# Transposes of the next token group in one run of eight, and look-ups in runs of four, in an FFT-and-routed-FFN kernel

## The chip, the cores and the metric

One core of a Trainium2 chip runs the whole program. The metric is the device time of one execution in microseconds; the time of a kernel is the median of its runs.

## What is computed

The reference filters eight sequences of 2496 rows by 256 columns in the frequency domain, then sends every filtered row through one of eight experts, each of which takes exactly 2496 rows:

```python
X = np.fft.rfft(x, axis=1)
y = np.fft.irfft(X * F, n=x.shape[1], axis=1).reshape(N, D)      # N = 19968, D = 256
logits = y @ w_gate
for idx in np.argsort(-logits.flatten()):                        # best (token, expert) first
    tok, e = idx // E, idx % E
    if assigned[tok] < 0 and counts[e] < N // E:
        assigned[tok], counts[e] = e, counts[e] + 1
for e in range(E):
    out[assigned == e] = np.maximum(y[assigned == e] @ w1[e], 0) @ w2[e]
```

## The kernel before

The first 400 us are the transforms (class Fft). They leave the filtered rows in device memory (xs) and the gate's logits on chip (lg). From about 420 us on the experts follow one another (class Ffn), and beside each expert the routing for the next ones runs (class Route): one search fixes which expert is closed next and at which logit, and a second part works out which rows belong to it.

**An expert.** Its 2496 rows are gathered by index in 20 tiles of 128 (the last has 64), four tiles to a group, five groups. `gather` issues a group's four indirect transfers on GpSimd's queue into the tiles xg. `turn(e, g, h)` transposes half a group: two tiles of two blocks, four transposes on TensorE (L839) into the PSUM tile ptr, then a cast by ScalarE (L842, hi) and a difference by VectorE (L843, lo), since float32 is carried as a sum of two rounded parts. `first(g, f)` makes one of the eight chunks of a group's hidden layer: six matmuls of up to 512 columns into the PSUM tile pz (L861), ScalarE's Relu into the high part (L867), VectorE's difference into the low part (L869, L872 in the last group). The second layer makes four row tiles per group: 24 matmuls of 256 columns each into py (L904), a copy by ScalarE (L914) and an indirect store (L915). One chunk of the next group stands before the first row tile and one before the fourth (ORD).

pz and ptr share one set of four PSUM buffers, tag "c". In `firsts` the next group is turned in two halves, before chunk 3 and before chunk 5 (TF); the second half is followed by the gather of the group after. The next expert's first group is turned by `hook` in the last group, one half after row tile 1 and one after row tile 2.

**The routing.** `counts` compares the logits with up to nine thresholds (Gm, L553, VectorE), counts by 11 to 13 matmuls (L561) and a few VectorE steps, and sums over partitions by a matmul with ones (L574). Eleven rounds make a search. `places` then finds the rows of the expert that was closed: for each of five pieces of its list, VectorE makes a comparison GE (L764) and four look-ups follow on TensorE (L771), in pairs. A pair writes one tile pr; VectorE takes loc from it (L772), ScalarE sums two Signs (L775, two instructions each), and VectorE takes ex (L776). All these small PSUM tiles have the name "rt" and two buffers, tag "a".

TensorE's order in this stage is the program's order. `Ffn.run` yields after a few matmuls, with the time they take; `Pump.feed` adds that to a clock and lets the routing go on by one step as soon as the step's lag has passed. `yield 'p', LO[2]` in `places` is such a step: the second pair of a piece comes 1.4 us of that clock after the first. The other engines' order is chosen by a scheduler.

Of the kernel before, what the change touches and what calls it, by code (L numbers as in the profile page):

```python
# [21 lines left out]
LAGS = [(1.6, 1.2), (1.9, 1.2), (2.4, 1.4), (2.2, 1.3), (2.2, 1.2), (2.6, 1.2), (2.6, 1.2), (2.6, 1.2)]  # L22
LO, M0, M1, M7 = (2.6, 1.2, 1.4), 3.5, 4.9, 6.9
TU0, TU, PACE = 1.1, 1.15, 5
ORD, TF = (1, 0, 0, 1), (3, 5)
I1, C0 = 5, -2
V1, V1D, V2, V3, VP, AC = 8, 0.5, 3, 2, -1, 6.5
Z0, ZS = 21, 4.6
# [434 lines left out]
class Route:  # L463
# [283 lines left out]
    def places(s, ph, tab, BE, xid, oid):  # L747

        nc, wp = s.nc, s.wb
        v = lambda n, sh, dt=F32, bufs=2: wp.tile(sh, dt, name=n, bufs=bufs)  # L750
        BC, dt = v("BC", [117, 5]), v("dt", [117, 180], F16)
        s.penal(2)
        yield 'o', 1.8
        s.penal(2)
        pd = s.ps.tile([128, 180], F32, name="rt", tag="a", bufs=2)
        nc.tensor.matmul(pd[:117], s.tri[:, 118:], tab, start=True, stop=True)
        nc.vector.tensor_copy(dt, pd[:117])
        ex, loc, js = v("ex", [128, 20, 2]), v("loc", [128, 20]), v("js", [128, 20])
        t1, t7 = v("t1b", [128, 20]), v("t7", [128, 4, 7])
        for ch in range(5):  # L760
            ts = slice(4*ch, 4*ch + 4)
            GE, t2 = v("GE", [117, 512], F16), v("t2", [128, 4])
            nc.vector.tensor_scalar(BC[:, ch:ch+1], BE, -512.0 * ch, None, op0=OP.add)
            nc.vector.tensor_scalar(GE, s.iota, BC[:, ch:ch+1], None, op0=OP.is_ge)  # L764
            yield 'o', LO[0] if ch == 0 else LO[1]
            s.penal(2)
            for t in range(0, 4, 2):
                u = slice(4*ch + t, 4*ch + t + 2)
                pr = s.ps.tile([128, 2, 180], F32, name="rt", tag="a", bufs=2)
                for h in range(2):  # L770
                    nc.tensor.matmul(pr[:, h], GE[:, 128*(t+h):128*(t+h)+128], dt, start=True, stop=True)  # L771
                nc.vector.tensor_tensor(loc[:, u], s.sidx[:, u], pr[:, :, S], op=OP.subtract)  # L772
                for h in range(2):
                    c = 4*ch + t + h
                    nc.scalar.activation(s.junka, pr[:, h, :S], AF.Sign, bias=loc[:, c:c+1], scale=-1.0, accum_out=js[:, c:c+1])  # L775
                nc.vector.tensor_scalar(ex[:, u], pr[:, :, S+1:S+3], MID, None, op0=OP.add)  # L776
                if t == 0:
                    yield 'p', LO[2]
                    s.penal(8)
            nc.vector.tensor_scalar(js[:, ts], js[:, ts], 0.5, S / 2, op0=OP.mult, op1=OP.add)  # L780
            x = nc.vector.scalar_tensor_tensor(xid[:, ts], ex[:, ts, 0], float(S), js[:, ts], op0=OP.mult, op1=OP.add)
            if ch == 0:
                s.last = x.ins
            nc.vector.tensor_tensor(t7, js[:, ts].unsqueeze(2).to_broadcast([128, 4, 7]),
                                    s.k22.unsqueeze(1).to_broadcast([128, 4, 7]), op=OP.is_ge)
            nc.vector.tensor_reduce(t1[:, ts], t7, axis=AX.X, op=OP.add)
            nc.vector.tensor_tensor(t2, js[:, ts], ex[:, ts, 1], op=OP.add)
            nc.vector.scalar_tensor_tensor(oid[:, ts], t1[:, ts], float(N - G), t2, op0=OP.mult, op1=OP.add)
            yield 'g', ch


class Ffn:
# [52 lines left out]
    def run(s, e, pump, hook):  # L845

        nc = s.nc
        ids = pump.out[e]
        out_rows = s.out
        _, ((w1h, w1l), (w2h, w2l)) = s.wt[e]  # L850
        hs = {}

        def first(g, f):
            n = min(512, CAP - 512*g)
            xh, xl = s.xT[e, g]
            p = s.ps.tile([128, 512], F32, name="pz", tag="c", bufs=4)
            m = 0
            for k in range(2):
                sl = slice(1024*k+128*f, 1024*k+128*f+128)
                for w, x in ((w1h, xh), (w1h, xl), (w1l, xh)):  # L860
                    nc.tensor.matmul(p[:, :n], w[:, sl], x[:, k, :n], start=m == 0, stop=m == 5)  # L861
                    m += 1
                yield 0.65 * n / 512
            hl = s.wp.tile([128, 1024], F32R, name="hl", bufs=NH)
            hs.setdefault(g, []).append(hl)
            h, l = (hl[:, 512*k:512*k+512] for k in range(2))
            s.lasta = s.R.relu = nc.scalar.activation(h[:, :n], p[:, :n], AF.Relu).ins  # L867
            if g < 4:
                s.R.low = nc.vector.scalar_tensor_tensor(l[:, :n], p[:, :n], 0.0, h[:, :n].bitcast(F32), op0=OP.max, op1=OP.subtract).ins  # L869
            else:  # L870
                for a, b, c in ((384, n, n), (0, 384, 512)):
                    s.R.low = nc.vector.scalar_tensor_tensor(hl[:, c:c+b-a], p[:, a:b], 0.0, h[:, a:b].bitcast(F32), op0=OP.max, op1=OP.subtract).ins  # L872

        def firsts(g, count):
            for f in range(len(hs.get(g, ())), min(8, len(hs.get(g, ())) + count)):
                if g + 1 < 5:
                    if f == TF[0]:
                        s.turn(e, g + 1, 0)
                    if f == TF[1]:
                        s.turn(e, g + 1, 1)  # L880
                        if g + 2 < 5:
                            hook(('g', g + 2))
                yield from first(g, f)

        hook(('g', 1))
        for g in range(5):
            n = min(512, CAP - 512*g)
            yield from firsts(g, 8)
            if g == 4:
                hook('last')  # L890
            if g == 0:
                hook('w2')
            for t in range(4):
                if g < 4:
                    yield from firsts(g + 1, ORD[t])
                w = min(128, n - 128*t)
                p = s.ps.tile([128, D], F32, name="py", tag="b", bufs=2)
                half = w == 64
                hi, lo, both = slice(128*t, 128*t+w), slice(512+128*t, 512+128*t+w), slice(384, 512)
                terms = ((both, w2h), (hi, w2l)) if half else ((hi, w2h), (hi, w2l), (lo, w2h))  # L900
                m = 0
                for f in range(8):
                    for a, b in terms:
                        nc.tensor.matmul(p[:a.stop-a.start], hs[g][f][:, a], b[:, 256*f:256*f+256],  # L904
                                         start=m == 0, stop=m == 8 * len(terms) - 1, skip_group_check=half)
                        m += 1
                    if f in ((3,) if half else (1, 3, 5)):
                        yield 0.65
                y = s.wp.tile([128, D], F32, name="y", bufs=4)
                if half:  # L910
                    nc.scalar.copy(y[:w], p[w:])
                    nc.vector.tensor_tensor(y[:w], p[:w], y[:w], op=OP.add)
                else:
                    s.lasta = nc.scalar.copy(y, p).ins  # L914
                st = nc.gpsimd.indirect_dma_start(  # L915
                    out=out_rows, out_offset=bass.IndirectOffsetOnAxis(ap=ids[1][:w, 4*g+t:4*g+t+1], axis=0),
                    in_=y[:w], in_offset=None)
                for o in s.scat:
                    s.tc.declare_no_dep(st.ins, o.ins, reason="each token has one place")
                s.scat.append(st)  # L920
                if t in (1, 2) and g == 4:
                    hook(t)
                yield 0.65


def emit(tc, i, out):
    nc = tc.nc
    with ExitStack() as st:
# [100 lines left out]
        with tc.manual_schedule(engines={mybir.EngineType.PE}):  # L1029
            for e in range(8):  # L1030
                pump.limit = e + 1
                def hook(what):
                    if what == 'w2':
                        flush(8)
                    elif isinstance(what, tuple):
                        gather(e, what[1])
                    elif e < 7:
                        if what == 'last':
                            gather(e + 1, 0)
                            flush(4)  # L1040
                        else:
                            W.turn(e + 1, 0, what - 1)
                for pe in W.run(e, pump, hook):
                    pump.feed(pe)
                    n += 1

                    if split and n % PACE == 0:
                        with tc.issue_after(W.lasta):
                            W.split(*split.pop(0))
# [85 lines left out]
```

## Time and profile before

| | us |
|---|---|
| median of three runs | 1422.91 (1422.52 to 1426.01) |
| profiled execution, time | 1421.42 |
| profiled execution, span | 1419.6 |
| TensorE busy | 1377.5 (97%) |
| VectorE busy | 891.6 (63%) |
| ScalarE busy | 673.7 (47%) |
| GpSimd busy | 484.6 (34%) |

The rows come from the profiled execution, whose time is its span and 1.8 us around it. PE is TensorE, PEld its weight loads, DVE VectorE, ACT ScalarE, POOL GpSimd. A matmul's duration runs from its start to the end of its drain; matmuls are pipelined, so what one costs is the distance from its start to the start of the next. The idle time in brackets names what ended it.

### The profile page before, as it was taken

The numbers are of one execution on the slowest core, as the hardware profiler recorded it, in microseconds if no ns is written. First come the engines' busy times: TensorE is split into PE (matmuls) and PEld (weight loads), VectorE is DVE, ScalarE is ACT, GpSimd is POOL, SyncE is SP. The second block draws the span as 40 slices with busy tenths as digits, with TensorE's granted clock in tenths as the row PEclk, the third lists the DMA queues.
The fourth block names the chain that finished last, engine by engine and source line by source line (L and its number), as shares of the span: only waits on it lengthen the run. The fifth ranks groups of instructions, "written<-read, shape, count | busy, mean of one in ns | idle before, by whom it ended". The sixth has DMA issues, their size and how long they took to land.

```text
span 1419.6 us, 27158 instructions
## 1 busy us (share of the span) xinstructions
PE 1377.5 (97%) x10338; PEld 1208.9 (85%) x10338; DVE 891.6 (63%) x2548; ACT 673.7 (47%) x1638; POOL 484.6 (34%) x538
## 2 busy tenths in 40 slices
PE   9999999999959999999999999999999999999998
PEld 8898898976427898898888889889898999899988
DVE  5577676775537778668766876876967635423231
ACT  6766766645454346326325534533623635423232
POOL 3443343431023226323521732433324323323312
PEclk9999999999989999999999999999999999999999
DMA  9665664537881022102212212112111321111100
GB/s 374 242 226 178 209 214 137 155 143 251 300 294 64 31 78 70 44 27 94 62 40 75 68 49 82 53 43 98 50 38 49 127 67 51 47 42 51 40 20 29
DMA packets 56531, 153.10 MB, mean 108 GB/s; under 512 B 9409, under 2 KB 29905, under 8 KB 52817
## 3 DMA queue, kind: packets, MB, share of 16 engines
q1 hardware_dynamic: 28072, 69.46, 14.0%
q0 software_dynamic: 18416, 60.37, 12.9%
q10 hardware_dynamic: 9913, 21.53, 4.3%
q8 instruction: 82, 1.34, 0.4%
q14 instruction: 48, 0.39, 0.1%
HBM read 88.32 MB, written 63.06 MB: 107 GB/s over the span
## 4 chain that ended last, share of the span: by engine, by line
PE 43%; issue 5%; DVE 3%; POOL 1%; ACT 1%; DMA 0%; POOLq 0%; DVEq 0%; ACTq 0%
PE py L904 21%; PE pz L861 19%; PE ptr L839 2%; PE rt L561 1%; POOL out L915 1%; DVE hl L872 1%; PE rt L771 1%; DVE w1l L819 0%; DVE tmp L640 0%; DVE tmp L642 0%; DVE M L638 0%; DVE ar L644 0%; ACT junka L775 0%; ACT hl L867 0%; DMA out<-y,oid 0%
## 5 line engine op out<-in xcount | busy, mean ns | idle before, releaser
L904 PE MATMUL py<-w1h,hl 128*128 128x256 f32 x2496 | 483.8, 286 | 1.0 <-DVE hl L872 1.0
L904 PEld LDWEIGHTS py<-w1h,hl 128*128 128x128 f32 x2496 | 401.7, 191 | 3.6 <-DVE hl L872 1.4
L904 PE MATMUL py<-w1l,hl 128*128 128x256 f32 (+1 forms) x1280 | 358.9, 282 | 0.0
L915 POOL DMA_INDIRECT out<-y,oid x160 | 167.1, 1045 | 496.3 <-ACT y L914 448.3
L867 ACT ACTIVATE hl<-pz 128x512 fp32r<-128x512 f32 (+1 forms) x320 | 187.9, 588 | 230.9 <-PE pz L861 204.1
L861 PE MATMUL pz<-xo,w0h 128*128 128x512 f32 (+1 forms) x640 | 264.2, 413 | 4.0 <-DVE hl L869 2.5
L869 DVE SCALAR_TENSOR_TENSOR hl<-pz,hl 128x512 fp32r<-128x512 f32 x256 | 175.2, 687 | 135.9 <-ACT hl L867 134.6
L861 PE MATMUL pz<-xo,w0l 128*128 128x512 f32 (+1 forms) x640 | 248.9, 389 | 0.0
L861 PE MATMUL pz<-z,w0h 128*128 128x512 f32 (+1 forms) x640 | 248.8, 389 | 0.0
L904 PEld LDWEIGHTS py<-w1l,hl 128*128 128x128 f32 (+1 forms) x1280 | 241.0, 188 | 1.9
L825 POOL DMA_INDIRECT xg<-xs,xid x160 | 170.3, 1064 | 137.1 <-issue 50.6
L914 ACT COPY y<-py 128x256 f32<-128x256 f32 x152 | 56.5, 372 | 298.7 <-PE py L904 264.5
L861 PEld LDWEIGHTS pz<-xo,w0l 128*128 128x128 f32 x640 | 120.9, 189 | 24.1
L861 PEld LDWEIGHTS pz<-xo,w0h 128*128 128x128 f32 x640 | 121.7, 190 | 22.2 <-DVE hl L869 3.0
L861 PEld LDWEIGHTS pz<-z,w0h 128*128 128x128 f32 x640 | 121.8, 190 | 15.7 <-DVE z L843 0.6
L219 ACT COPY Y<-p 64x240 f32<-64x240 f32 (+1 forms) x302 | 115.2, 381 | 30.0 <-PE p L213 22.9
L237 POOL TENSOR_TENSOR P<-P 128x256 f32<-128x256 f32 x80 | 58.6, 732 | 164.0 <-DVE P L235 163.8
L553 DVE TENSOR_TENSOR Gm<-M,thr 117x1232 bf16<-117x1232 f32 (+2 forms) x80 | 105.4, 1328 | 0.2
L213 PE MATMUL p<-cS,xr 117*128 117x120 f32 x688 | 94.0, 276 | 3.4 <-ACT Y L219 1.5
L213 PEld LDWEIGHTS p<-cS,xr 117*128 117x128 f32 x688 | 85.4, 191 | 7.6 <-ACT Y L219 4.3
L229 PE MATMUL p<-cW,Y 128*128 128x128 f32 x640 | 88.4, 276 | 0.6 <-DVE Q L236 0.6
L229 PEld LDWEIGHTS p<-cW,Y 128*128 128x128 f32 x640 | 80.0, 191 | 5.7 <-issue 3.9
(218 smaller groups left out, 1982.3 us busy)
## 6 DMA issues: line engine op xcount, KB each, us to landing
z<-zd SPq DMA_DIRECT2D x26, 600.0 KB
zd<-zt SPq DMA_DIRECT2D x60, 256.0 KB
xs<-xo ACTq DMA_DIRECT2D x18, 600.0 KB
xr<-x SPq DMA_DIRECT2D x6, 1536.0 KB
xr<-x SPq DMA_DIRECT2D x6, 1216.0 KB
zd<-zt ACTq DMA_DIRECT2D x20, 256.0 KB
xs<-xo SPq DMA_DIRECT2D x8, 600.0 KB
xr<-x SPq DMA_DIRECT2D x8, 512.0 KB
```

The costliest lines, as they stand in the source:

```text
L213: s.lastmm = nc.tensor.matmul(p[:, q-q0, :120], xv[:, q-24*h], s.cS1, start=True, stop=True).ins
L219: c = (nc.vector.tensor_copy if (t == 5 if b else cp) else nc.scalar.copy)(dst, src)
L229: nc.tensor.matmul(p[:, k], s.Y1[b][:, 4*g+k, dh*128:dh*128+128], s.cW[:, 4*g+k], start=True, stop=True)
L237: nc.gpsimd.tensor_tensor(P[:, :, :64], P[:, :, :64], P[:, :, 64:], op=OP.subtract)
L553: nc.vector.tensor_tensor(Gm[:, s0:s1, :m], s.M[:, s0:s1].unsqueeze(2).to_broadcast([117, s1 - s0, m]), thr[:117].unsqueeze(1).to_broadcas ...
L825: s.lastg = s.nc.gpsimd.indirect_dma_start(out=xg[:n], out_offset=None, in_=s.xs, in_offset=bass.IndirectOffsetOnAxis(ap=ids[0][:n, t:t+1] ...
L861: nc.tensor.matmul(p[:, :n], w[:, sl], x[:, k, :n], start=m == 0, stop=m == 5)
L867: s.lasta = s.R.relu = nc.scalar.activation(h[:, :n], p[:, :n], AF.Relu).ins
L869: s.R.low = nc.vector.scalar_tensor_tensor(l[:, :n], p[:, :n], 0.0, h[:, :n].bitcast(F32), op0=OP.max, op1=OP.subtract).ins
L904: nc.tensor.matmul(p[:a.stop-a.start], hs[g][f][:, a], b[:, 256*f:256*f+256], start=m == 0, stop=m == 8 * len(terms) - 1, skip_group_check ...
L914: s.lasta = nc.scalar.copy(y, p).ins
L915: st = nc.gpsimd.indirect_dma_start(out=out_rows, out_offset=bass.IndirectOffsetOnAxis(ap=ids[1][:w, 4*g+t:4*g+t+1], axis=0), in_=y[:w], i ...
```

## The change

Three edits. In `places`, the step between the two pairs of a piece is kept for the first search alone (ph is the search's number); in the later seven the four look-ups stand together. In `firsts`, both halves of the next group are turned before chunk 4, and the gather of the group after follows there. At the end of an expert, both halves of the next expert's first group are turned after row tile 1.

```diff
-ORD, TF = (1, 0, 0, 1), (3, 5)
+ORD, TF = (1, 0, 0, 1), 4
...
                 if t == 0:
-                    yield 'p', LO[2]
+                    if ph == 0:
+                        yield 'p', LO[2]
                     s.penal(8)
...
                 if g + 1 < 5:
-                    if f == TF[0]:
-                        s.turn(e, g + 1, 0)
-                    if f == TF[1]:
-                        s.turn(e, g + 1, 1)
+                    if f == TF:
+                        for h in range(2):
+                            s.turn(e, g + 1, h)
                         if g + 2 < 5:
                             hook(('g', g + 2))
...
-                if t in (1, 2) and g == 4:
-                    hook(t)
+                if t == 1 and g == 4:
+                    hook('turn')
...
                         else:
-                            W.turn(e + 1, 0, what - 1)
+                            for h in range(2):
+                                W.turn(e + 1, 0, h)
```

In the changed kernel the lines behind the first edit have numbers one higher, up to `firsts`.

TensorE, a group of the last expert, before, at the second half's transposes (x4 counts equal rows in a row):

```order
L861 MATMUL pz<-xo,w0h 128x512
L861 MATMUL pz<-z,w0h 128x512
L861 MATMUL pz<-xo,w0l 128x512
L839 MATMUL ptr<-id,xg 128x128 x4
L861 MATMUL pz<-xo,w0h 128x512
L861 MATMUL pz<-z,w0h 128x512
```

and in the changed kernel:

```order
L862 MATMUL pz<-xo,w0h 128x512
L862 MATMUL pz<-z,w0h 128x512
L862 MATMUL pz<-xo,w0l 128x512
L840 MATMUL ptr<-id,xg 128x128 x8
L862 MATMUL pz<-xo,w0h 128x512
L862 MATMUL pz<-z,w0h 128x512
```

The two runs of four of a group have become one run of eight.

TensorE at the end of the second expert, before, where the last pair of look-ups but one meets the counts of the next search:

```order
L904 MATMUL py<-w1h,hl 128x256
L771 LDWEIGHTS GE
L771 MATMUL rt<-dt,GE 128x180
L771 LDWEIGHTS GE
L771 MATMUL rt<-dt,GE 128x180
L561 LDWEIGHTS Gm
L561 MATMUL rt<-A,Gm 48x80
```

and in the changed kernel:

```order
L904 MATMUL py<-w1h,hl 128x256
L771 LDWEIGHTS GE
L771 MATMUL rt<-dt,GE 128x180
L771 LDWEIGHTS GE
L771 MATMUL rt<-dt,GE 128x180
L771 LDWEIGHTS GE
L771 MATMUL rt<-dt,GE 128x180
L771 LDWEIGHTS GE
L771 MATMUL rt<-dt,GE 128x180
L561 LDWEIGHTS Gm
L561 MATMUL rt<-A,Gm 48x80
```

The counts now stand behind a run of four.

VectorE in the search beside the fourth expert, before, around a run of transposes (Gm is the search's comparison, hl the eviction of a chunk, z that of a ptr tile):

```order
L594 TENSOR_TENSOR km<-km,di 128x1
L553 TENSOR_TENSOR Gm<-M,thr 117x1232
L869 SCALAR_TENSOR_TENSOR hl<-pz,hl 128x512
L843 TENSOR_TENSOR z<-ptr,xo 128x2x256
L869 SCALAR_TENSOR_TENSOR hl<-pz,hl 128x512
```

and in the changed kernel:

```order
L594 TENSOR_TENSOR km<-km,di 128x1
L553 TENSOR_TENSOR Gm<-M,thr 117x1232
L870 SCALAR_TENSOR_TENSOR hl<-pz,hl 128x512 x2
L844 TENSOR_TENSOR z<-ptr,xo 128x2x256 x2
```

Both chunks that stand ahead of the eight transposes, and both ptr tiles, now follow the Gm.

## Rows read from the trace of the kernel before

**Rows 1.** The page, section 1: busy us, share of the span and instructions per engine.
```profile
PE 1377.5 (97%) x10338; PEld 1208.9 (85%) x10338; DVE 891.6 (63%) x2548; ACT 673.7 (47%) x1638; POOL 484.6 (34%) x538
```

**Rows 2.** Waits of PE, 440 to 1420 us: total us, times, longest.
```profile
PE py L904 <- DVE hl L872: 1.0, 1, 1.0
PE rt L771 <- DVE t L569: 0.9, 1, 0.9
PE rt L561 <- DVE ex L776: 0.6, 2, 0.3
...
PE pz L861 <- DVE hl L869: 0.2, 1, 0.2
```

**Rows 3.** Tile ptr: count, duration min/median/max in ns, first and last start.
```profile
L839 PE MATMUL ptr<-id,xg x320: 222/272/473, 420.2 to 1378.1; 128*128 128x128 f32 x152, 64*128 64x64 f32 x8
```

**Rows 4.** Timeline of PE, 487.1 to 488.8 us: start, duration in us, instruction, count.
```profile
487.60 0.40 PE L861 MATMUL pz<-xo,w0l 128*128 128x512 f32 x1
487.83 0.60 PE L839 MATMUL ptr<-id,xg 128*128 128x128 f32 x4
488.19 0.48 PE L861 MATMUL pz<-xo,w0h 128*128 128x512 f32 x1
488.50 0.39 PE L861 MATMUL pz<-z,w0h 128*128 128x512 f32 x1
```

**Rows 5.** Line 771: count, duration min/median/max in ns.
```profile
L771 PE MATMUL rt<-dt,GE x160: 237/242/375, 400.6 to 1223.8; 117*128 117x180 f16 x160
```

**Rows 6.** Timeline of PE, 652.4 to 653.2 us.
```profile
652.67 0.33 PE L771 MATMUL rt<-dt,GE 117*128 117x180 f16 x2
652.79 0.36 PE L904 MATMUL py<-w1h,hl 128*128 128x256 f32 x1
652.99 0.29 PE L904 MATMUL py<-w1l,hl 128*128 128x256 f32 x1
```

**Rows 7.** Timeline, 686 to 688.2 us, one pair and its readers.
```profile
686.09 0.33 PE L771 MATMUL rt<-dt,GE 117*128 117x180 f16 x2
...
686.46 0.16 DVE L772 TENSOR_TENSOR loc<-sidx,rt 128x2 f32<-128x2 f32 x1 [0.58 <-PE rt L771]
...
687.77 0.16 DVE L776 TENSOR_SCALAR ex<-rt 128x4 f32<-128x4 f32 x1 [0.67 <-ACT junka L775]
```

**Rows 8.** Timeline of PE, 678.3 to 680.3 us, counts right behind a pair.
```profile
679.02 0.58 PE L561 MATMUL rt<-A,Gm 117*48 117x80 bf16 x11 [0.32 <-DVE ex L776]
```

**Rows 9.** Timeline, 1330.6 to 1332 us, eviction of a chunk that ends at 1330.80.
```profile
1330.80 0.60 PE L839 MATMUL ptr<-id,xg 128*128 128x128 f32 x4
1331.00 0.60 ACT L867 ACTIVATE hl<-pz 128x512 fp32r<-128x512 f32 x1 [0.79 <-PE pz L861]
...
1331.63 0.69 DVE L869 SCALAR_TENSOR_TENSOR hl<-pz,hl 128x512 fp32r<-128x512 f32 x1 [0.69 <-ACT hl L867]
```

**Rows 10.** Groups by line, VectorE, 560 to 1420 us: busy us, mean ns, idle before.
```profile
L553 DVE TENSOR_TENSOR Gm<-M,thr 117x1232 bf16<-117x1232 f32 (+1 forms) x50 | 74.0, 1481 | 0.1
```

**Rows 11.** Timeline, 430.3 to 439 us, and the window of the lower clock.
```profile
430.45 0.60 PE L839 MATMUL ptr<-id,xg 128*128 128x128 f32 x4
433.36 0.50 PE L861 MATMUL pz<-xo,w0h 128*128 128x512 f32 x1 [2.31 <-DVE hl L869]
...
435.35 0.68 DVE L869 SCALAR_TENSOR_TENSOR hl<-pz,hl 128x512 fp32r<-128x512 f32 x1
...
438.55 0.48 PE L861 MATMUL pz<-xo,w0h 128*128 128x512 f32 x1
...
434.80:437.80 3.00, 3.00 (x9) 1.98 (x7) 3.00 (x5) 0.60 (x1) 0.00 (x0) 0.51 0.00 0
```

**Rows 12.** Timeline, 664 to 681 us: a gather's issue and the first transposes behind it.
```profile
664.24 0.95 POOL L825 DMA_INDIRECT xg<-xs,xid  x1 [0.30 <-PE py L904]
...
680.35 0.60 PE L839 MATMUL ptr<-id,xg 128*128 128x128 f32 x4
```

**Rows 13.** Window 560 to 690 us: length, busy us of PE, PEld, DVE, ACT, POOL, clock, DMA.
```profile
560.00:690.00 130.00, 128.66 (x934) 113.64 (x933) 93.90 (x308) 56.07 (x142) 52.04 (x47) 1.00 0.19 62
```

## The prediction

> **What bounds the kernel now.** I read the page's totals first: TensorE is busy for 1377.5 us, 97% of the span, no other engine for more than 892 [rows 1]. The change touches the expert stage only, from 420 us on, so I read that stage's waits of TensorE next: between 440 us and the end they come to 3.8 us in seven entries, from 1.0 down to 0.2 [rows 2]. The stage is a queue of matmuls without holes. It follows that an instruction taken from TensorE's queue, or a pause between two kinds of matmul, is worth its full length; that moving work on VectorE, ScalarE or GpSimd is worth nothing by itself; and that any new wait in TensorE's queue is paid in full. So the sum has two sides: what eight in a row and four in a row save between kinds of matmul, and what waits the longer runs make.
>
> **The transposes: almost nothing saved.** There are 320 transposes in 80 calls of turn [rows 3]. The first 8 stand together in both kernels; the other 78 calls become 39 runs of eight. What does one run of four cost? Before the run, matmuls of pz start every 0.23 us (487.60, 487.83); the first transpose starts where the next pz would have; the next pz starts 0.36 us later, and the one behind it another 0.31, 0.08 more than 0.23 [rows 4]. A run of four costs 0.36 + 0.08 = 0.44 us. What of it is the change of kind, which merging saves? The four last 0.60 us together and one lasts 0.272 [rows 3, 4], so they start every (0.60 - 0.272)/3 = 0.109 us, and four times that is 0.437. The rest is nothing to 0.02 us by the rounding of the rows: 39 merges save 0 to 0.8 us. I take 0.2, near the rows' own difference.
>
> Here a rule speaks for a larger gain. The Trainium skill (TensorE: Matmul & The Clock Gate, "Back-to-back issue gap") gives about 81 ns for each matmul of 128 columns in a sustained stream of loads and matmuls; were the added four transposes of each run to settle there, 39 x 4 x (0.109 - 0.081) = 4.4 us would go, by an estimate from that page. The rows show 0.109 from the second transpose on, with no trend that I can see in four, so the sum goes by the rows, and a faster second half is a rival below.
>
> **The look-ups: a small gain.** 160 matmuls of GE make 80 pairs [rows 5]; the ten pairs of the first search stay, 70 pairs become 35 runs of four. A pair between py matmuls, which start every 0.12 us: the next py starts 0.12 after the pair, the one behind it 0.20 after that [rows 6], so a pair costs 0.12 + 0.08 = 0.20 us. The pair lasts 0.33 and one 0.242 [rows 5, 6], so the second starts 0.088 after the first, and two such steps are 0.176; 0.024 is the change of kind. Were the spacing 180 columns at the upper level, 2.4 GHz, or 0.075 us, it would be 0.05. 35 merges save 0.8 to 1.75 us; I take 1.2.
>
> **A new wait: the search's counts behind a run of four.** pr tiles come from the two buffers "rt", which the counts use too. A matmul of counts (L561) needs the buffer used two tiles earlier. Behind a pair that is the pair before, long read; behind a run of four it is the first half of that very run. How long does a pair take to be read? Look-ups at 686.09, loc at 686.46, then two Signs with their accumulator reads, ex from 687.77 to 687.93: 1.84 us [rows 7]. The run of four takes 4 x 0.088 = 0.35 on TensorE, so counts that stand right behind it wait about 1.5 us, and everything in TensorE's queue behind them waits too. The order of the changed kernel has that in two places (at the ends of the first and the second expert), and in three more there are 1.4 us of other matmuls between, which leaves about 0.1 each. That is 2 x 1.5 + 0.3 = 3.3 us new. Against it the old waits of this kind go, since the look-ups of a list now end before the next search's counts begin: 0.9 (look-ups behind the counts' buffer) and 0.6 (counts behind ex) [rows 2]; one of the latter is at 679.02 [rows 8]. Net +1.8 us. Bounds: with waits of the 0.32 us that the old place shows [rows 8], 0.6 - 1.5 = -0.9; with ScalarE held up by a 0.60 us eviction between each pair of Signs and the order twice as unlucky, +4.
>
> **A thinner cover: the buffers of pz.** pz and ptr share four buffers. Before, a run of four stands between chunks 2 and 3 of a group's eight (a chunk is one call of first, six matmuls of 0.23) and another between 4 and 5; the tile that needs its buffer soonest comes 2 x 1.37 + 0.44 = 3.2 us after the end of the one that used it. Now two ptr tiles follow chunk 3, chunks 4 and 5 need the buffers of 2 and 3, and those ended 1.37 + 0.88 = 2.25 us earlier. A quiet eviction takes 1.52 us: a chunk ends at 1330.80, VectorE has subtracted it by 1331.63 + 0.69 [rows 9]. The cover was 1.7 us, now it is 0.73. In the last two experts that costs nothing. While a search runs, VectorE makes a Gm comparison of 1.48 us in ten of a search's rounds, 50 in the five searches from 560 us on [rows 10]. One Gm fits into 1.7, not into 0.73. VectorE's new order puts a Gm right ahead of the one or two evictions before a run of eight in six of the 24 places; a Gm that has just begun makes TensorE wait 1.48 - 0.73 = 0.75, one that is nearly done nothing, so 6 x 0.375 = 2.3 us. Bounds 0 (Gm always early) and 5 (each of the six in full, and the four-buffer delay handed on once). I take 1.9, a little under the mean, since at some of them the Gm starts before the chunk has ended.
>
> **The start of the stage.** TensorE's longest stall, 2.31 us behind VectorE at 431, stands at the first run of four that moves, and the granted clock falls to 0.51 (the lower level, 1.2 GHz) from 434.8 to 437.8, after the stall [rows 11]. Now chunk 3 runs at 430.45 in place of the four, the eight transposes wait for the same evictions, and chunk 4 waits for the eviction that ends at 435.35 + 0.68 = 436.03 [rows 11]. Chunk 4 then ends at 437.4 at full clock or 438.8 at the lower, where before it ended, with its eight transposes, at 438.55. I take -0.5, bounds -1.2 and +0.7.
>
> Nothing else has a price. The last transposes of each expert (after the second y tile of group 4, where they were after the second and the third) find their rows gathered: at the boundary in the rows the fourth of them was issued 16 us ahead of the first transposes [rows 12]. The gather of group g + 2 is issued one chunk sooner on GpSimd's queue, which is 34% busy [rows 1].
>
> **Sum:** -0.2 - 1.2 + 1.8 + 1.9 - 0.5 = +1.8 us on the profiled execution's 1421.42, 1423.2. That execution lies 1.5 under the median of the runs, 1422.91, so the predicted time is **1424.7 us**: no change that a measurement can tell (about 0.3%, 4.3 us, since the runs before spread over 3.5).
>
> **Rivals.** *Faster: the longer runs flow better.* If the second four transposes settle to 128 columns at 2.4 GHz, 0.053 us, the least a run at the clock's upper level can take, 39 x 4 x 0.056 = 8.7 us go: 1414 us. Half of that would be 1418.6. Against it: 0.109 in every run I looked at. A milder way to the same side is that none of the two waits comes and the seven old ones go too: -0.2 - 1.2 - 0.5 - 3.8, 1417.2. Together 0.14.
>
> *Slower: pz's buffers become the bound in each search.* If VectorE, in its fixed order, has a Gm or a reduction in front of chunk 2 or 3 at half of the 24 runs of eight, and 0.75 us is lost at each, 9 us are added and with the counts' wait 11: 1434 us. It decides where the eviction takes more than 2.25 us. For it: VectorE is 63% busy overall and 93.9 of 130 us, 72%, beside a search [rows 1, 13], and the stall at 431 is of just this kind. Against it: only 0.2 us of waiting on L869 after 440 us. Short of that, both waits at their upper bounds give 1422.9 - 1.9 + 9 = 1430. Together 0.24.
>
> *That the runs are not formed* can be left out: the order of the changed kernel has the eight and the four adjacent in TensorE's queue at all 39 and 35 places.
>
> **How the numbers follow.** The forecast, within 0.3%: 0.62. The range takes in the lower bounds of the waits with both savings (1422.9 - 0.8 - 1.75 - 0.9 = 1419.5, a bit lower with the start) and the upper bounds with small savings (1422.9 + 4 + 5 - 1 = 1430.9, both at once being unlikely): 1419 to 1430.
>
> **What would show it.** Each step has its line: eight transposes lasting 0.27 + 7 x 0.109 = 1.04 us and costing 0.88; four look-ups costing 0.37 where two pairs cost 0.40; two waits of 1.5 us of L561 on ex of L776; waits of pz on L869 of some tenths at runs of eight while a search runs, none after 1230 us. I am wrong if the eight cost under 0.8, if no wait on ex shows, or if pz waits for VectorE by more than 5 us in all.

## The result, and the profile after

The changed kernel takes **1442.21 us** (median of four runs, 1441.19 to 1444.16), the kernel before 1424.06 beside it (four runs, 1422.52 to 1426.01): a ratio of 1.0144, 95% interval 1.0131 to 1.0158, so some 19 to 22 us slower. The forecast, 1424.7 with a range up to 1430, was wrong.

The runs were taken in seven sessions, and the kernel before itself takes 1422 to 1424 us in four of them ("1422 sessions", this one included) and 1440 to 1445 in three ("1440 sessions"), so each ratio is against the kernel before in its own session.

The page of the kernel after, its first section (busy us, share of the span and instructions; [rows 1]):

```profile
span 1439.4 us, 27170 instructions
...
PE 1380.1 (96%) x10338; PEld 1213.9 (84%) x10338; DVE 891.3 (62%) x2548; ACT 672.9 (47%) x1638; POOL 482.9 (34%) x538
```

The span is 19.8 us longer, TensorE's busy time only 2.6: the engine does the same work and stands idle for it. The first and the last matmul of py bound the stage that the change touches; they start at 444.37 and 1414.04 before:

```profile
444.37 0.28 PE L904 MATMUL py<-w1h,hl 128*128 128x256 f32 x1
...
1414.04 0.28 PE L904 MATMUL py<-w1l,hl 128*64 128x256 f32 x1
```

and after at

```profile
443.54 0.36 PE L904 MATMUL py<-w1h,hl 128*128 128x256 f32 x1
...
1433.81 0.28 PE L904 MATMUL py<-w1l,hl 128*64 128x256 f32 x1
```

969.67 us have become 990.27, so all of the loss, 20.6 us, lies there and none in the start. What TensorE waited for after 440 us in the kernel after (us in total, times, longest; [rows 2] are those of before):

```profile
PE rt L771 <- DVE ex L776: 13.6, 11, 3.9
PE rt L561 <- DVE ex L776: 4.2, 3, 2.3
PE pz L862 <- DVE hl L870: 2.3, 2, 1.7
PE rt L561 <- DVE Gm L553: 0.8, 2, 0.5
PE py L904 <- DVE hl L873: 0.5, 1, 0.5
PE pz L862 <- DVE z L844: 0.4, 1, 0.4
```

21.8 us where it was 3.8. The first line is most of the loss, and it wasn't in the sum: look-ups that wait for ex, VectorE's last reading of a buffer "rt", of the **run of look-ups before them**. The longest of these eleven waits shows how. Timeline of the kernel after, the run of look-ups at 783.20, its readers, what VectorE does between them, and the next run:

```profile
783.20 0.49 PE L771 MATMUL rt<-dt,GE 117*128 117x180 f16 x4
...
783.55 1.61 DVE L638 TENSOR_REDUCE M<-lg 117x176 f32<-117x1408 f32 x1
...
786.79 0.14 DVE L772 TENSOR_TENSOR loc<-sidx,rt 128x2 f32<-128x2 f32 x1
...
787.72 1.61 DVE L640 TENSOR_TENSOR tmp<-lg,M 117x1408 f32<-117x1408 f32 x1
...
788.78 0.19 ACT L775 ACTIVATION_READ_ACCUMULATOR junka<-rt,loc 128x1 f32 x1
789.25 0.69 DVE L553 TENSOR_TENSOR Gm<-M,ic 117x528 bf16<-117x528 f32 x1
...
792.14 0.21 DVE L776 TENSOR_SCALAR ex<-rt 128x4 f32<-128x4 f32 x2
...
792.34 0.48 PE L771 MATMUL rt<-dt,GE 117*128 117x180 f16 x4 [3.88 <-DVE ex L776]
```

TensorE wrote the two buffers by 783.7. VectorE, whose order is fixed, first makes the reduction M that begins the next search, an eviction and a low part of the weights; loc comes 3.6 us after the look-ups. ScalarE's Signs end at 788.97. Then tmp, Gm, three evictions and a weight stand ahead of ex, which ends at 792.35, 9.15 us after the look-ups. The next run of four came 5.3 us after the one before it and waited.

The long waits also cost speed. The clock's windows of the kernel after, behind the waits of 2.27 us (which ends at 681.16) and 3.88 us (columns as in [rows 13]):

```profile
793.00:797.00 4.00, 4.00 (x23) 4.00 (x23) 4.00 (x13) 2.88 (x11) 2.75 (x3) 0.57 0.14 37
681.00:684.00 3.00, 2.83 (x20) 2.73 (x21) 1.20 (x11) 0.94 (x4) 0.00 (x0) 0.50 0.02 5
```

TensorE ran there mostly at the lower level, 1.2 GHz: 0.43 x 4 + 0.5 x 2.83 = 3.1 us of work lost. Waits of 18.0 more and these 3.1, less the 1.75 that the merged runs save (below), make 19.4 of the 20.6.

### The profile page after: what moved, and what is told of

Read it like the earlier page. It is cut to its first block, busy times and chain, and to the rows that moved or that the text cites. A ratio compares the mean times of both kernels' runs of the same rounds, so it can differ in the third digit from the quotient of the medians.

```text
span 1439.4 us, 27170 instructions
## 1 busy us (share of the span) xinstructions
PE 1380.1 (96%) x10338; PEld 1213.9 (84%) x10338; DVE 891.3 (62%) x2548; ACT 672.9 (47%) x1638; POOL 482.9 (34%) x538
## 4 chain that ended last, share of the span: by engine, by line
PE 54%; DVE 7%; issue 5%; ACT 2%; POOL 1%; DMA 1%; POOLq 0%; DVEq 0%; ACTq 0%
PE py L904 26%; PE pz L862 24%; PE ptr L840 2%; PE rt L561 2%; POOL out L915 1%; DVE hl L870 1%; ACT junka L775 1%; DVE w1l L820 1%; DVE hl L873 1%; DVE Gm L553 1%; ACT lg L745 1%; ACT hl L868 1%; DVE tmp L642 1%; PE rt L771 1%; DVE M L638 0%
## 5 line engine op out<-in xcount | busy, mean ns | idle before, releaser
L862 PE MATMUL pz<-xo,w0h 128*128 128x512 f32 (+1 forms) x640 | 260.0, 406 | 4.7 <-DVE hl L870 2.3
```

## The experiments

**The halves apart.** e1 is the change without its look-up edit, e2 without its transposes' (the hook at an expert's end likewise put back).

```diff
                 if t == 0:
-                    if ph == 0:
-                        yield 'p', LO[2]
+                    yield 'p', LO[2]
                     s.penal(8)
```

```diff
-ORD, TF = (1, 0, 0, 1), 4
+ORD, TF = (1, 0, 0, 1), (3, 5)
...
-                    if f == TF:
-                        for h in range(2):
-                            s.turn(e, g + 1, h)
+                    if f == TF[0]:
+                        s.turn(e, g + 1, 0)
+                    if f == TF[1]:
+                        s.turn(e, g + 1, 1)
```

> The transposes in runs of eight alone; the look-ups stay in pairs with the step of 1.4 between them. Theory (the 18 us are look-ups waiting for the two rt buffers, the eights are harmless): 1421 to 1427 us, waits of L771 on ex at most 2 us in all. Rival A (the shorter cover of pz's buffers around eight transposes costs it): 1432 us or more, with the added waits on pz's and ptr's evictions.

> The look-ups in runs of four alone; the transposes stay in runs of four. Theory: 1437 to 1445 us, waits of L771 on ex of 10 us or more and of L561 on ex of about 4, as in the changed kernel. Rival A (eights cost it): 1422 to 1427 us. Rival C (each half harmless, only both together cost): 1422 to 1428 us.

Both fell in a 1440 session: eight alone 1455.7 against 1440.61, ratio 1.0098 (1.0071 to 1.0124), which I had not expected; four alone 1460.83, 1.0142 (1.0111 to 1.0173), with 13.5 us of look-ups behind ex. Repeated, they fell in a 1440 session again:

> Eight transposes in a row, look-ups in pairs as before, once more beside another set of runs of the kernel before. Theory A (all of the loss is in the look-ups' buffers): no change, ratio 0.998 to 1.002, waits of TensorE from 440 us on under 6 us. Rival (the eight cost VectorE's and ScalarE's order something, as the first run of this edit, 1.0098, would have it): ratio above 1.006 with 8 us or more of waits on hl, loc or X.

> Look-ups in runs of four, transposes in two runs of four as before. Theory A: the whole loss is here: ratio 1.012 to 1.017, waits on ex of L771 and L561 of 15 to 20 us together. Rival (half of the loss is in the transposes): 1.005 to 1.010.

1.0076 (1.0060 to 1.0091) and 1.0148 (1.0133 to 1.0162). Four alone is as theory A has it, with 16.7 us on ex; eight alone is as its rival has it, with 8.6 us of waits on X, a VectorE step of each count. The third time it was a 1422 session:

> Eight transposes in a row, pairs as before. If the kernel before takes about 1422 us here: theory A gives ratio 0.998 to 1.002, waits of TensorE after 440 us under 6 us, and no idle time of VectorE that nothing releases; the rival (the eight cost something themselves) a ratio above 1.004. If the kernel before takes about 1440 us here, 1.007 to 1.011 again.

> Runs of four look-ups, transposes as before. Where the kernel before takes about 1422 us: theory A gives ratio 1.011 to 1.016 and 14 to 20 us of waits on ex; the rival, half of the loss from the transposes, 1.004 to 1.009.

Eight alone: 1424.64 against 1421.69, **1.0025** (1.0015 to 1.0035), +2 to +5 us, between the two expectations. Its largest waits of TensorE after 440 us:

```profile
PE rt L561 <- DVE ex L776: 2.4, 3, 1.8
PE pz L861 <- DVE loc L772: 1.6, 2, 1.1
PE py L903 <- DVE hl L872: 1.0, 1, 1.0
PE rt L771 <- DVE t L569: 0.9, 1, 0.9
PE rt L574 <- DVE X L571: 0.4, 2, 0.2
```

In all 6.6 us against 3.8: one count now waits 1.8, and pz waits 0.6 more. Four alone: 1446.11, **1.0167** (1.0149 to 1.0185), +21 to +26 us, just above the range of theory A; its largest waits:

```profile
PE rt L771 <- DVE ex L776: 12.0, 10, 4.1
PE rt L561 <- DVE ex L776: 4.5, 3, 2.3
PE pz L862 <- DVE z L844: 2.5, 2, 1.5
PE py L905 <- DVE hl L873: 1.8, 2, 1.5
PE pz L862 <- DVE hl L870: 1.7, 1, 1.7
```

The loss is the look-ups'. In company the eight cost nothing more: both edits together took 1.0154 (e6) in such a session. That e14 is even slower than both edits is mostly the clock: its mean granted share is 0.57 from 792 to 800 us and 0.66 in 553 to 558, 908 to 913 and 1024 to 1029, some 7 us of TensorE's work by these means, where the kernel after lost 3.1.

**Controls.**

> Control: the kernel before, unchanged, profiled beside the others of this call. If the +14 us of eight transposes alone came from the change, this trace has under 5 us of TensorE waits between 440 us and the end, like the trace of before; if it came from whatever makes the kernel before take 1440 instead of 1423 there, this trace shows the same stalls of VectorE and ScalarE (some us at 446 to 459 and at 570 to 579) and 12 to 20 us of TensorE waits.

> Control: the changed kernel, unchanged. Theory A (look-ups wait for buffers that VectorE releases late): the waits of L771 and L561 on ex are 15 to 20 us again, the ratio to the kernel before 1.010 to 1.018. If the size of the loss depends on disturbances that come with a chip, the ratio is outside that.

> Control: the kernel before, for its trace. On a chip where it takes about 1440 us, the idle time of VectorE and ScalarE that nothing in the profile releases should be over 15 us each after 440 us, as in the other kernels there; if it is near zero, those stalls belong to the changed orders and not to the chip.

All three fell in 1422 sessions: 1422.2, ratio 1.0005 (0.9996 to 1.0014); 1444.11, ratio 1.0154 (1.0139 to 1.0169); and 1422.63 in one run. The waits on ex of the kernel after came back to a tenth, 13.6 and 4.3 us, so they belong to the order of the program and not to chance. So e5 and e15 never showed the kernel before in a 1440 session, which is what half of their expectation was about.

**The pace.** The step that the change removes also shortens the time from piece to piece. e3 is the kernel after with 1.4 us more behind each piece, e4 the kernel before, in pairs, with 1.4 us less (e12 and e17 repeat it).

```diff
-        u[0] = s.clock + s.lag[k](t)
+        u[0] = s.clock + s.lag[k](t) + (1.4 if k == 'g' and u[1] else 0)
```

> The whole change, with 1.4 of the pump's clock added to the lag behind each piece of a list, so that the runs of four follow one another about 7.0 us apart, as TensorE's order counts, where the change has 5.4 and the kernel before had 7.5 from pair to same pair. Theory, pace (a run of four comes before VectorE and ScalarE have read the two rt buffers of the one before): waits of L771 on ex under 4 us, 1421 to 1429 us. Rival B (four at once need both buffers and load ScalarE with four Signs in a row, whatever the pace): waits stay at 10 us or more, 1436 us or more.

> The kernel before, with pairs and runs of four transposes, and 1.4 of the clock taken off the lag behind each piece: the same pair of two pieces is about 6.0 us apart instead of 7.5. Theory, pace: waits of L771 on ex of 4 to 12 us appear with pairs too, 1428 to 1437 us. Rival B (it takes runs of four): waits as before, under 2 us, 1422 to 1427 us.

> The kernel before with pairs, but 1.4 us less behind each piece, so that a piece takes as long as in the changed kernel while the pairs stay apart. If the pace alone makes look-ups outrun the buffers: waits of L771 on ex 8 to 12 us, ratio 1.005 to 1.009. If it needs four in a row: waits under 3 us, ratio 0.999 to 1.002.

> Pairs as before, 1.4 us less behind each piece. Where the kernel before takes about 1422 us: if a piece's shorter time is enough to outrun the buffers, 8 to 12 us of waits of L771 on ex and a ratio of 1.004 to 1.009, about half of the loss of the runs of four; if four in a row are needed, under 3 us and 0.999 to 1.002.

All four fell in 1440 sessions. Pairs with the short piece: 1.0068 (1.0041 to 1.0095), 1.0036 (1.0022 to 1.0050) and 1.0036 (1.0021 to 1.0052), each with 8 to 11 us of look-ups behind ex; in e4

```profile
PE rt L771 <- DVE ex L776: 9.7, 8, 3.5
```

where e9, in pairs at the old pace in a 1440 session too, has

```profile
PE rt L771 <- DVE ex L776: 0.2, 1, 0.2
```

So the shorter pace is enough to make these waits, without four in a row. It is not the whole price: the short piece costs 9 and 4 us in the two sessions in which the fours alone cost 20 and 22. Fours with the long piece: 1.0214 (1.0188 to 1.0240), far outside what I expected; the look-ups' waits fell to 2.5 us, as expected, but the pieces now reached further into the next search, and its counts came right behind runs of four:

```profile
PE rt L561 <- DVE ex L776: 16.1, 8, 3.3
PE pz L862 <- DVE hl L870: 4.6, 5, 1.5
PE rt L771 <- DVE ex L776: 2.5, 2, 2.1
```

A wait for the same two buffers, under another name.

**ex earlier.** In e7 (kernel after) and e8 (kernel before) ex is written ahead of the Signs, so that ScalarE's second Sign is the last reader.

```diff
                 nc.vector.tensor_tensor(loc[:, u], s.sidx[:, u], pr[:, :, S], op=OP.subtract)
+                nc.vector.tensor_scalar(ex[:, u], pr[:, :, S+1:S+3], MID, None, op0=OP.add)
                 for h in range(2):
...
-                nc.vector.tensor_scalar(ex[:, u], pr[:, :, S+1:S+3], MID, None, op0=OP.add)
```

> The changed kernel with ex moved to the place behind loc, ahead of the two Signs, so that the last reader of a look-up's buffer is ScalarE's second Sign. Theory A, that ex stands behind other work in VectorE's fixed order and releases the buffer late: waits on ex of L771 and L561 go from about 18 us to under 3, at most 6 us come back as waits on ScalarE's Signs, and the time falls by 8 to 15 us against the changed kernel (ratio to the kernel before 1.002 to 1.008). Rival, that loc is as late as ex, so that the Signs are late too: the waits move to junka of L775 nearly whole, over 10 us, and the ratio stays above 1.010.

> The kernel before with the same move of ex. Theory A: pairs have a piece's other pair between a buffer's uses, little waits there, so under 2 us are to be had: ratio 0.998 to 1.001. Rival, that any new order of VectorE's work costs several us whatever it is meant to do: ratio above 1.004.

In a 1422 session: e7 1436.2 us, 8 less than the kernel after in the same session (e6), 1.0096 (1.0081 to 1.0110); e8 1422.19, 1.0003 (0.9994 to 1.0011). In e7 no wait on ex is left, but more than I allowed came back on the Signs:

```profile
PE rt L561 <- ACT junka L776: 7.1, 5, 2.6
PE pz L862 <- DVE hl L870: 3.3, 3, 2.2
PE rt L771 <- ACT junka L776: 2.7, 5, 1.0
```

So 8 of the 22 us were ex's place in VectorE's order. What is left on these buffers, 9.8 us, waits for the Signs, which need loc first and follow one another on ScalarE; which of the two holds them up more was not separated. The result lies between the two expectations.

**The runs spaced.** e11 is the kernel after, e16 and e18 (one kernel) have its look-ups with the old transposes; all with ex early, with more room from run to run (0.8 us in e11, 1.4 in the others), and with the counts kept 2.2 us away from a run of four.

```diff
-        u[0] = s.clock + s.lag[k](t)
+        u[0] = s.clock + s.lag[k](t) + (1.4 if k == 'g' and u[1] else 0)
...
             if u[0] <= s.clock:
                 s.step_side(u)
+                if u[1] and u[0] > s.clock + 2.9:
+                    s.due = max(s.due, s.clock + 2.2)
```

> The changed kernel with ex early, 0.8 us more between the runs of four, and the counts of the next search kept 2.2 us of TensorE's clock away from a run of four. In TensorE's order all but two of the 35 runs then have at least 2.7 us of other matmuls behind them before the next tile rt. Theory A (the loss is the waits for the two rt buffers and nothing else): waits on ex and on junka under 3 us together, ratio 0.998 to 1.002, no loss left. Rival (the waits move to the search's other steps, as they did with the slower pace alone): waits of L561 or L574 on VectorE over 8 us, ratio above 1.006.

> Runs of four look-ups, transposes as before, ex early, 1.4 us more between the runs of four and the counts kept 2.2 us of TensorE's clock away from them: in TensorE's order at least 6 us from run to run and 2.9 us from a run to the next counts. Where the kernel before takes about 1422 us: theory A (the waits are the whole loss) gives under 3 us of waits of L771 and L561 on ex, loc and junka, ratio 0.998 to 1.003, against 1.0167 without the spacing. Rival (a run of four loads VectorE and ScalarE so that other waits take their place): waits on hl, X or Gm over 8 us and a ratio above 1.007.

> The same kernel as in e16. Where the kernel before takes about 1422 us: theory A (the waits for the two buffers are the whole loss) gives 0.998 to 1.004 with waits on ex, loc and junka under 3 us and under 6 us on hl; the rival (spaced runs of four still push VectorE's evictions or the search late) over 1.007 with more than 8 us of waits on hl, X, t or Gm. Where the kernel before takes about 1440 us: 1.010 to 1.017 again, and the question stays open.

e11 and e16 fell in 1440 sessions: 1.0096 (1.0082 to 1.0111) and 1.0134 (1.0099 to 1.0170), both misses. In e11 10.4 us of waits on junka are left. In e16 the look-ups' and counts' waits for buffers are nearly gone (1.6 us on junka, none on ex), but pz waits 8.4 us on hl, a sign of the rival, and engines stand idle where nothing in the profile releases them. Two of the largest of VectorE's waits of e16 after 440 us that are put down to no instruction:

```profile
DVE hl L870 <- issue: 16.8, 10, 9.3
DVE t L569 <- issue: 9.8, 4, 2.5
```

So e18 ran the same kernel once more, and in a 1422 session it takes **1420.37 us against 1422.38, a ratio of 0.9983** (0.9974 to 0.9993). All of TensorE's waits after 440 us:

```profile
PE rt L561 <- DVE Gm L553: 1.8, 4, 0.7
PE pz L862 <- DVE ex L773: 0.8, 1, 0.8
PE pz L862 <- ACT hl L868: 0.7, 1, 0.7
PE pz L862 <- DVE hl L870: 0.3, 1, 0.3
PE py L905 <- DVE hl L873: 0.3, 1, 0.3
```

3.9 us, as in the kernel before, and none for a buffer that a look-up holds. The same four in a row that cost 24 us in e14 gain 2 us here: the rival, that fours load the other engines too much, falls for the 1422 sessions, and the waits for the two buffers were the loss. It took the three edits together: ex early alone gave back 8 us (e7), and more room from run to run alone moved the wait to the counts (e3). This is the one version that beats the kernel before, by 1 to 4 us, in one 1422 session; the whole change with its runs spaced (e11) was timed in a 1440 session alone.

## Why the prediction was wrong, step by step

**The bound** was right, and the loss obeys it: TensorE's queue has no slack, and every new wait was paid in full.

**The transposes** were right to the hundredth. Timeline of the kernel after, a run of eight between chunks:

```profile
461.67 1.04 PE L840 MATMUL ptr<-id,xg 128*128 128x128 f32 x8
462.46 0.47 PE L862 MATMUL pz<-xo,w0h 128*128 128x512 f32 x1
462.77 0.39 PE L862 MATMUL pz<-z,w0h 128*128 128x512 f32 x1
```

0.79 + 0.08 = 0.87 us, twice the old 0.44: nothing saved. From (1.04 - 0.272)/7 the spacing is still 0.110 us in a run of eight, so the rival that built on a faster second half falls. The Trainium skill (TensorE: Matmul & The Clock Gate, "Back-to-back issue gap") gives about 81 ns for a matmul of 128 columns in a sustained stream; this trace does not agree, with its 110 ns.

**The look-ups' saving** was at its better bound. A run of four in the kernel after:

```profile
536.47 0.48 PE L771 MATMUL rt<-dt,GE 117*128 117x180 f16 x4
536.74 0.36 PE L904 MATMUL py<-w1h,hl 128*128 128x256 f32 x1
536.94 0.28 PE L904 MATMUL py<-w1l,hl 128*128 128x256 f32 x1
```

costs 0.27 + 0.08 = 0.35 us against 0.40 for two pairs: 35 x 0.05 = 1.75 us, where I took 1.2. e18, whose waits are those of the kernel before (3.9 us against 3.8), is 1.8 us shorter than the kernel before from the first py to the last (967.89).

**The new wait**, +1.8 us in the sum for counts behind a run of four, is the step that failed, in two ways.

- *Who waits.* I asked only which counts stand behind a run of four. The next run of four needs the same two buffers, and that wait, 13.6 of the 18 us, was not in the sum. The removed step was priced as a pause between matmuls and not as what it was for the buffers: time. From the trace's rows of L771 after 525 us, a buffer came back to TensorE after 7.3 us or more before the change (median 7.9), and after 5.1 or more with it (median 5.9). e4, e12 and e17 make the wait by a shorter pace alone. With the time given back in e3 (6.6 or more, median 7.4) it falls from 13.6 to 2.5 us; in e18 (6.6 or more, median 7.5), where ex is early too, it is gone.
- *How long a buffer is held.* I took 1.84 us from one pair at 686 [rows 7], a quiet place. Beside the beginning of a search VectorE has other things first. The kernel before already had this: a pair, and the next one that needs its buffer,

```profile
900.48 0.33 PE L771 MATMUL rt<-dt,GE 117*128 117x180 f16 x2
...
907.96 0.15 DVE L776 TENSOR_SCALAR ex<-rt 128x4 f32<-128x4 f32 x1
...
908.26 0.33 PE L771 MATMUL rt<-dt,GE 117*128 117x180 f16 x2
```

  stand 7.78 us apart, and ex ends 7.63 us after the first. Of the 70 pairs after 525 us 18 were held for more than 5.4 us. The kernel before lost nothing by it, with 0.15 us to spare here, and so no view of waits showed it. With the change the longest of these times is 9.68. The pace was the cover, and I let it go without a price.

None of the three signs by which I meant to see that I was wrong came (eight that cost under 0.8, no wait on ex, over 5 us of pz behind VectorE): none of them stood for a look-up that waits.

For the counts alone the step was nearly right: 3.3 us predicted, 4.2 measured in three waits (1.41, 2.27, 0.57), where a buffer was held longer than 1.84.

**pz's cover** came out at the predicted size, +1.9, by luck: pz's waits after 440 us went from 1.0 (0.2 on hl [rows 2], 0.5 on loc and 0.3 on r in the same view) to 2.7, so by 1.7. The mechanism is there, an eviction that comes too late for the shorter cover at a run of eight:

```profile
1010.01 1.04 PE L840 MATMUL ptr<-id,xg 128*128 128x128 f32 x8
...
1011.24 1.61 DVE L638 TENSOR_REDUCE M<-lg 117x176 f32<-117x1408 f32 x1
...
1014.14 0.50 PE L862 MATMUL pz<-xo,w0h 128*128 128x512 f32 x1 [1.70 <-DVE hl L870]
```

But what delayed it was not what I counted, a Gm at six places: 1.70 us stand here behind the reduction M of a search's beginning, 0.61 at 780.33 behind ScalarE, which was busy with other work, and only 0.36 at 755.85 behind a Gm. Nor does the shorter cover alone give the 1.7: with the eight alone (e13) pz's waits grew by 0.6, and with the fours alone (e14), where that cover is untouched, they are 4.2. **The start** can't be told: from the first transposes to the first py it takes 24.2, 22.5 and 22.0 us in three traces of the kernel before and 23.2 and 22.4 in two of the kernel after.

**The clock** had no term: 3.1 us behind the two longest waits. With it the sum is 18.0 + 3.1 - 1.75 = 19.4 of the 20.6 measured; 1.2 us are not placed.

The rival that ended on the slower side, pz's buffers, had the right mechanism (a late eviction in VectorE's fixed order outlasts a cover that was cut) at the wrong buffers.

## What to carry to other kernels

A pause in a hand-made order is also the time in which a buffer comes free: before taking one out, write down for each buffer of its loop the time from use to next use, before and after, and the longest time from write to last read, not one quiet example. No waits in a view means only that the cover holds, not that it is thick; the rows of the last reader behind the busiest stretch of its engine show how thick. Four in a row were not in themselves what cost here: with more room between the runs, ex early and the counts held off they gained 2 us (e18). But room between the runs alone only moved the wait to the next user of the same buffers (e3), so every user of a buffer has to be in the list.

## What the runs showed of the hardware

A long wait can be paid partly behind it, where no view of waits has it. Behind the wait of 3.88 us the granted clock was 1.00 from 792 to 793 us, 0.74 in the next microsecond and 0.50 to 0.55 up to 797; in e6, the same program, it had fallen to 0.50 within the same wait and stayed there up to 798. In e13 a wait of 1.76 us was followed by the same (0.50 from 1027 to 1029), while 1.70 us at 1014 in the kernel after was not.

The 1440 sessions I had not expected at all: the same kernel before takes 16 to 23 us longer there, and the ten traces taken in them (e1 to e4, e9 to e12, e16, e17) show VectorE and ScalarE idle for 19 to 50 us each after 440 us, put down to no instruction, where VectorE in the 1422 sessions has none of this. Eight alone lost 0.8 to 1.0% there in place of 0.25%, and the spaced fours 1.3% in place of a gain; the fours alone lost 1.4 to 1.5%, about the 1.7% of the other kind. Whether this belongs to a chip is not shown: the record gives the number 0 to the chip of e9 to e12 and to that of e18, one session of each kind. What holds the engines up there was not found, and the kernel before was never profiled in such a session, so it is open whether its own loss there is of this kind.
